# Holding the last three zero blocks until the last batch's ranks, half a weight matrix more ahead of the gathers, and a bank of its own for the score pieces

## The chip, the cores and the metric

The kernel runs on one core of one Trainium2 chip. The metric is the device time of one launch in microseconds (us), the median of several runs. The engines are named as in the profile: PE (TensorE), PEld (its weight loads), DVE (VectorE), ACT (ScalarE), POOL (GpSimd) and SP (SyncE, which here only issues DMAs). POOL issues DMAs too, into a queue of its own; all queues share the core's 16 DMA engines.

## The reference

```python
def reference(**kwargs):
    ...
    attn_out = _attn_ref(**attn_kwargs)
    B, H, S, D = attn_out.shape
    x = np.ascontiguousarray(attn_out.transpose(0, 2, 1, 3)).reshape(B * S, H * D)
    return _moe_ref(x=x, **moe_kwargs)
...
    logits = x @ w_gate
    expert_idx = np.argmax(logits, axis=1)
    ...
    gate_w = probs[np.arange(N), expert_idx]
    out = np.zeros((N, D), dtype=np.float32)
    for e in range(E):
        ...
        if len(tok_idx) > capacity:
            gw = gate_w[tok_idx]
            keep = np.argpartition(-gw, capacity)[:capacity]
            tok_idx = tok_idx[keep]
        h = np.maximum(x[tok_idx] @ w1[e], 0.0)
        out[tok_idx] = gate_w[tok_idx, None] * (h @ w2[e])
```

Attention for 8 batches of 8 heads: 512 local tokens that see a window of 32 to each side and 32 global tokens, and the global tokens, which see all. Its rows (4352 of 512 numbers) go to a mixture of 8 experts: each token goes to its best expert, an expert keeps the 80 tokens with the highest gate, and all other rows of the output are zero.

## The kernel before

The program is one list of operations (`op`), each with the resources that it reads and writes and a due time. A planner (`Work.emit`) sorts them by due time, by readiness under rough costs and by free PSUM banks, and so fixes the order of the instructions on each engine. The chip keeps only this order and the true dependences of tiles; a resource that is only a name in the list (such as "rk21") moves an operation in the order and makes nothing wait on the chip.

Attention fills the first 197 us, batch by batch (line 1030 on): scores, exponentials, values, normalisation (`norm`), rows cast to bf16 in `xb` and written to a scratch tensor `x_scr` (`X_rows`). Beside it `gate_pieces(b)` picks the tokens of each batch: logits, the one-hot of the best expert (`oh`), the score split into bf16 pieces (`v7`), a transpose of both into one PSUM bank (T56, line 718), from which rows 0:56 are copied to `oh3T` and rows 32:56 to `S3T`; then five products `r_ps` (line 736) whose signs or comparisons, summed, give the rank of each token in its expert. For the last batch DVE compares pieces 0 and 4 (line 745), and ACT counts signs of pieces 1, 2 and 3 (line 750) and turns the sums of signs into counts (line 756: half of it plus 256). `d_ps` does the same for the global tokens and gives `rk2` (line 771). `rank` and `ohs` (lines 778, 779) turn ranks into a one-hot, a product and a merge with the lists so far give `idx`, the 80 token numbers of each expert.

Then the experts' stage. POOL gathers the 80 rows of each expert by indirect DMA (`gather`, line 1090); PE transposes them (`f_turn`, line 1109), multiplies by w1 in two halves (`f_up`, line 1122) and by w2 (`f_down`, line 1139); ACT scales the result by the gate, POOL scatters it to `out` (line 1156). I call the four transposes of expert e fx-e, the halves of w1 up-e-a and up-e-b, and the product with w2 y-e.

Weights come as fp32 from HBM and are cast to bf16 by the DMA, 1 MB of bf16 per matrix, on POOL's queue, in the order in which POOL issues them, into buffers that attention has finished with. Those in `wload` (line 1027) are issued before the gathers; the last of them is the first half of w1 of expert 6. Those in `wlate` follow among the gathers (line 1171): seven halves, the second half of w1 of expert 6 between the gathers of experts 1 and 2.

Zeros: 17 blocks of 512 KB are written to `out` on SP's queue (`zero`, line 389), 14 between loads of v and the last three at the end of SP's list (line 1080). The scatters wait until all have landed.

`warm` (line 1183) puts matmuls that nobody reads (line 1190, "unread") into the gaps that the planner expects on PE in the end stage.

Of the kernel before, what the change touches and what calls it, by code (L numbers as in the profile page):

```python
# [76 lines left out]
class Work:  # L77
# [10 lines left out]
    def at(self, due):  # L88
        self.due = due
# [131 lines left out]
def kernel(  # L221
# [49 lines left out]
    def bankS(name, shape=(P, 512), dt=FP32):  # L271
        return Bank("S", list(shape), dt, name)
# [48 lines left out]
    ones = cp.tile([cap, 1], BF16, name="ones")  # L321
    gq32 = wr[2][:, 0:4096].bitcast(FP32).rearrange("p (t b x) -> p t b x", t=2, b=B)
# [295 lines left out]
    def gate_pieces(b):  # L618
# [99 lines left out]
        T56 = bankS(f"T56_{b}", (56, 544), BF16)  # L718
# [7 lines left out]
        op([("D", 0.45), ("A", 0.6)], lambda e: copy_on(e, oh3T[0:56, 0:544], T56[:]), rd=[T56],  # L726
           wr=["oh3T"])
        op([("A", 0.6), ("D", 0.45)], lambda e: copy_on(e, S3T[0:24], T56[32:56, :]), rd=[T56], wr=["S3T"])
        step = 1 if last else 2
        for u in range(5):  # L730
# [25 lines left out]
        op([("A", 0.25)], lambda e: nc.scalar.activation(  # L756
            out=st["rk1"][:, 1:4:step], in_=st["rk1"][:, 1:4:step], func=AF.Copy, scale=0.5, bias=256.0),
            rd=[f"rk1{y}{u}" for u in range(1, 4, step)], wr=[f"rk1{y}{u}" for u in range(1, 4, step)])
# [226 lines left out]
    def f(e):  # L985
# [5 lines left out]
                                                       op0=ALU.mult, op1=ALU.add), rd=["second"], wr=["wsg"])  # L991
    at(-50)
# [23 lines left out]
    for t_ in (1, 0):  # L1016
# [12 lines left out]
              (175, 6, 0, 0, 2)]  # L1029
    wlate = [(6, 0, 2, 4), (6, 1, 0, 4), (6, 1, 4, 8), (7, 0, 0, 2), (7, 0, 2, 4), (7, 1, 0, 4), (7, 1, 4, 8)]  # L1030
# [197 lines left out]
```

## Time and profile before

| | |
|---|---|
| median of 3 runs | 249.5 us (248.96 to 249.52) |
| the profiled execution | 248.41 us, its span 246.5 us |
| PE busy, of the span | 211.8 us, 86% |
| DVE, ACT, POOL busy | 155.8, 149.7, 130.5 us |
| DMA | 51.90 MB written, mean 211 GB/s |
| granted clock of PE, mean | 0.976 |

The span is the time from the first to the last instruction; the rest of the execution's own time lies around it. Busy shares are means over stages with different limits; the stage that matters here is read in stretches of one or two microseconds. GB/s counts the bytes written: a weight that is cast from fp32 to bf16 counts with its bf16 bytes.

### The profile page before, as it was taken

Reading aid. Unit: us, or ns where it says so; the run is one execution under the profiler, and the core shown is the slowest. Engines: PE = TensorE matmul, PEld = TensorE weight load, DVE = VectorE, ACT = ScalarE, POOL = GpSimd, SP = SyncE. Lnnn points to the kernel's source line nnn. Section 1 sums busy time; section 2 is a strip of 40 time slices with the busy share of each in tenths; the row PEclk is TensorE's granted clock in tenths of the full one; section 3 lists DMA queues with packets and bytes.
Section 4 is the critical chain, followed back from the end, with each engine's and each line's share of the span. In section 5 each row is a group of like instructions: output and inputs, shape, how many; then the busy total and the mean of one; then the engine's idle time right before and its main releaser. Section 6 shows DMA issues by size and latency. Waiting matters only on the chain.

```text
span 246.5 us, 10141 instructions
## 1 busy us (share of the span) xinstructions
PE 211.8 (86%) x4337; PEld 166.5 (68%) x4354; DVE 155.8 (63%) x396; ACT 149.7 (61%) x312; POOL 130.5 (53%) x215
## 2 busy tenths in 40 slices
PE   0589589797999898999799989999999977679991
PEld 0567477585778677887688768777778654357760
DVE  7248377718979857777676767878877777221210
ACT  2469557918878786867575878868593435024431
POOL 8937245525468564572547643516686330588331
PEclk9999979979999999999989999999999999999998
DMA  6999988999999999999997999997899999299971
GB/s 102 234 224 180 232 180 147 200 212 205 172 252 163 217 276 265 204 299 232 299 205 214 291 219 224 237 275 181 163 179 243 209 243 307 51 213 216 197 203 55
DMA packets 54798, 51.90 MB, mean 211 GB/s; under 512 B 42976, under 2 KB 43488, under 8 KB 53984
## 3 DMA queue, kind: packets, MB, share of 16 engines
q0 software_dynamic: 8896, 27.14, 59.6%
q1 hardware_dynamic: 45856, 24.11, 35.2%
q8 instruction: 34, 0.56, 0.9%
q14 instruction: 12, 0.10, 0.1%
HBM read 61.72 MB, written 14.68 MB: 310 GB/s over the span
## 4 chain that ended last, share of the span: by engine, by line
PE 60%; issue 13%; DVE 12%; POOL 7%; ACT 6%; POOLq 1%; DVEq 0%; ACTq 0%
PE o_ps L520 13%; PE o_ps L505 8%; PE T_ps L403 7%; PE x_ps L584 5%; PE l_ps L481 4%; PE lgT_ps L640 4%; PE r_ps L736 3%; PE og L551 3%; POOL out_dram L1156 2%; DVE qkT L266 2%; ACT eL L486 2%; PE T L723 2%; DVE xn L533 1%; PE Q_ps L460 1%; PE og L556 1%
## 5 line engine op out<-in xcount | busy, mean ns | idle before, releaser
L593 POOL CAST xb<-xn 128x512 bf16<-128x512 f32 x32 | 21.4, 669 | 44.2 <-DVE xn L533 36.8
L520 PE MATMUL o_ps<-vt,eL 128*64 128x65 f32 x1024 | 39.3, 231 | 3.0 <-issue 3.0
L486 ACT ACTIVATE eL<-l_ps 128x512 f32<-128x512 f32 x64 | 35.6, 609 | 5.5 <-PE l_ps L481 5.3
L520 PEld LDWEIGHTS o_ps<-vt,eL 128*64 128x64 f32 x1024 | 34.5, 143 | 6.6 <-issue 4.4
L491 DVE TENSOR_TENSOR eL<-eL,first 128x512 f32<-128x512 f32 x38 | 31.2, 844 | 7.5 <-ACT eL L486 7.3
L266 ACT COPY xT<-x_ps 128x512 f32<-128x512 f32 x30 | 17.6, 587 | 18.3 <-PE x_ps L584 18.3
L505 PE MATMUL o_ps<-vgb,eG 64*128 64x130 f32 x256 | 23.9, 303 | 4.4 <-issue 2.4
L533 DVE TENSOR_TENSOR xn<-o_ps,rec 128x512 f32<-128x512 f32 x32 | 22.1, 692 | 3.1
L505 PEld LDWEIGHTS o_ps<-vgb,eG 64*128 64x128 f32 x256 | 17.7, 190 | 8.3 <-issue 4.7
L266 ACT COPY qkT<-T_ps 128x1024 f16<-128x1024 f16 x21 | 21.4, 1020 | 3.0 <-PE T_ps L403 3.0
L266 POOL COPY vt<-vt 64x260 f32<-64x260 f32 (+2 forms) x30 | 22.1, 750 | 1.9 <-DMA vt<-in_v_l_dram 0.6
L403 PE MATMUL T_ps<-ident,qk 128*64 128x128 f16 x512 | 22.1, 239 | 0.1
L266 DVE COPY qkT<-T_ps 128x1024 f16<-128x1024 f16 x11 | 13.5, 1224 | 12.0 <-PE T_ps L403 11.9
L584 PE MATMUL x_ps<-identf,xn 128*128 128x128 f32 x128 | 20.4, 283 | 0.4
L403 PEld LDWEIGHTS <-qk 128*64 128x64 f16 x512 | 18.0, 122 | 1.9 <-issue 1.0
L584 PEld LDWEIGHTS x_ps<-identf,xn 128*128 128x128 f32 x128 | 15.2, 143 | 2.9
L481 PE MATMUL l_ps<-qkT 64*128 64x64 f16 x512 | 14.5, 198 | 2.7 <-DVE qkT L266 1.9
L266 ACT COPY vt<-vt 64x1040 f32<-64x1040 f32 (+2 forms) x18 | 16.1, 900 | 0.5 <-DMA vt<-in_v_l_dram 0.2
L491 POOL TENSOR_TENSOR eL<-eL,first 128x512 f32<-128x512 f32 x10 | 12.0, 1198 | 7.7 <-ACT eL L486 5.9
L481 PEld LDWEIGHTS <-qkT 64*128 64x128 f16 x512 | 10.8, 99 | 7.7 <-issue 4.1
L745 DVE SCALAR_TENSOR_TENSOR junk<-r_ps,second 128x512 bf16<-128x512 f32 x23 | 15.6, 680 | 0.5 <-PE r_ps L736 0.5
L532 DVE RECIPROCAL rec<-o_ps 128x8 f32<-128x8 f32 x32 | 6.4, 201 | 13.3 <-PE o_ps L520 13.2
(174 smaller groups left out, 444.5 us busy)
## 6 DMA issues: line engine op xcount, KB each, us to landing
out_dram<-zt SPq DMA_DIRECT2D x17, 512.0 KB, 9.7
vt<-in_v_l_dram SPq DMA_DIRECT2D x64, 128.0 KB, 4.9
wr<-in_moe_w_dram POOLq DMA_DIRECT2D x6, 1024.0 KB, 9.9
qk<-in_q_l_dram POOLq DMA_DIRECT2D x8, 512.0 KB, 7.4
qk<-in_k_l_dram POOLq DMA_DIRECT2D x8, 512.0 KB, 7.6
x_scr<-xb SPq DMA_DIRECT2D x8, 512.0 KB, 7.8
qk<-in_moe_w_dram POOLq DMA_DIRECT2D x2, 1024.0 KB, 11.2
qkT<-in_moe_w_dram POOLq DMA_DIRECT2D x2, 1024.0 KB, 9.6
```

The lines of the kernel that those rows point to most:

```text
L266: (eng.copy if e == "A" else eng.tensor_copy)(out=out, in_=in_)
L403: nc.tensor.transpose(out=bk[64 * q:64 * q + 64, i, :], in_=qk16[b % 2][:, t, q, 8 * half + i, :], identity=ident16[:, :])
L481: mm(out=lps[s, k][:, 64 * t:64 * t + 64], lhsT=kv(s, j)[r, 64 * t:64 * t + 128], rhs=qv(s, j)[r, 64 * t + 32:64 * t + 96], start=k != 2, ...
L486: op([("A", 0.53)], lambda e, k=k, e_=e_: nc.scalar.activation(out=e_, in_=lps[s, k][:], func=AF.Exp, scale=scale), rd=[lps[s, k]], wr=[f" ...
L491: lambda e, e_=e_: engines[e].tensor_tensor(out=e_, in0=e_, in1=band, op=ALU.mult),
L505: mm(out=o[:, j, 130 * u:130 * u + 130], lhsT=eG[s % 2][r, q0:q0 + 128], rhs=vgb[r, s // 2, s % 2].rearrange("p h d -> p (h d)"), start=(u ...
L520: mm(out=ost[s, h][64 * odd:64 * odd + 64, k // 2, c:c + 65], lhsT=eL[s % 2][:, k, 64 * t:64 * t + 64], rhs=v[:, 4 * odd + u, k, :], start ...
L533: nc.vector.tensor_tensor(out=xn[:, s % 2, h].rearrange("p j u (k d) -> p j (u k) d", k=2), in0=o[:, :, :, 0:64], in1=rec[:].unsqueeze(3). ...
L584: nc.tensor.transpose(out=bk[:, c:c + 128], in_=xn[:, s % 2, h, j, u], identity=identf[:, :])
L593: op([("G", 0.65)], lambda e: nc.gpsimd.tensor_copy(out=xb[(s // 2) % 2][:, 2 * h:2 * h + 2, :, s % 2, :].rearrange("p u q (j d) -> p u q ...
L640: mm(out=lgt[32 * c:32 * c + 32, 0:P], lhsT=wg[:, f, :], rhs=xslot(2 * b + f // 2, c, f % 2), start=(f == 0), stop=(f == 3), skip_group_ch ...
L745: nc.vector.scalar_tensor_tensor(out=junk[:], in0=bk[:], scalar=0.0, in1=wst[:, 512 - 128 * u:1024 - 128 * u], op0=ALU.add, op1=ALU.is_gt, ...
```

## The change

- The last three zero blocks are to start later: SP first issues a DMA of 4 bytes (`word`) from `rk2` of the last batch, so that SP waits for it, and behind it the three blocks.
- The list ahead of the gathers takes the whole of w1 of expert 6. Six halves stay among the gathers, at other places.
- For the last batch the pieces of the score are transposed a second time, into a bank of their own (T24), from which `S3T` is copied by ACT, while DVE copies `oh3T` from T56.
- For the last batch the sums of signs are no longer turned into counts: `rk2` of columns 1 to 3 is doubled on DVE (line 786 of the changed kernel), and `ohs` compares with a table `rev5`, whose columns 1 to 3 hold 2 x - 512. Two operations on POOL make the table early on.
- `df` is kept in bf16 in all batches.

```diff
@@ gate_pieces @@
-        T56 = bankS(f"T56_{b}", (56, 544), BF16)
+        T24 = T56 = bankS(f"T56_{b}", (56, 544), BF16)
+        r24 = slice(32, 56)
+        if last:
+            T24, r24 = bankS(f"T24_{b}", (24, 544), BF16), slice(0, 24)
+
+            def f(e):
+                for u in range(5):
+                    n = P if u < 4 else SG
+                    nc.tensor.transpose(out=T24[:, 128 * u:128 * u + n], in_=st["vi"][0:n, u, 32:56],
+                                        identity=identb[0:n, 0:n])
+            op([("P", 0.3)], f, rd=["v7" + y, "identb"], new=[T24], mode="128x56", tail=0.2, room=1)
...
-        op([("A", 0.6), ("D", 0.45)], lambda e: copy_on(e, S3T[0:24], T56[32:56, :]), rd=[T56], wr=["S3T"])
-        step = 1 if last else 2
+        op([("A", 0.6)] if last else [("A", 0.6), ("D", 0.45)], lambda e: copy_on(e, S3T[0:24], T24[r24, :]), rd=[T24], wr=["S3T"])
...
-        op([("A", 0.25)], lambda e: nc.scalar.activation(
-            out=st["rk1"][:, 1:4:step], in_=st["rk1"][:, 1:4:step], func=AF.Copy, scale=0.5, bias=256.0),
+        if not last:
+            op([("A", 0.25)], lambda e: nc.scalar.activation(
+            out=st["rk1"][:, 1:4:2], in_=st["rk1"][:, 1:4:2], func=AF.Copy, scale=0.5, bias=256.0),
...
-            df = t("df", [P, 5, SG])
+            df = t("df", [P, 5, SG], BF16)
...
+            if last:
+                nc.vector.tensor_scalar(out=st["rk2"][:, 1:4], in0=st["rk2"][:, 1:4], scalar1=2.0, scalar2=None, op0=ALU.mult)
...
-            nc.vector.tensor_tensor(out=ohs[:], in0=(nat if b == 0 else rev).unsqueeze(1).to_broadcast([P, 5, cap]),
+            nc.vector.tensor_tensor(out=ohs[:], in0=rev5[:] if last else (nat if b == 0 else rev).unsqueeze(1).to_broadcast([P, 5, cap]),
@@ the constants @@
+        nc.gpsimd.tensor_copy(out=rev5[:, 0:5:4], in_=rev.unsqueeze(1).to_broadcast([P, 2, cap]))
+        nc.gpsimd.tensor_scalar(out=rev5[:, 1:4], in0=rev.unsqueeze(1).to_broadcast([P, 3, cap]), scalar1=2.0, scalar2=-512.0,
+                                op0=ALU.mult, op1=ALU.add)
+    op([("G", 0.9)], f, rd=["second"], wr=["rev5"])
@@ the weights @@
-              (175, 6, 0, 0, 2)]
-    wlate = [(6, 0, 2, 4), (6, 1, 0, 4), (6, 1, 4, 8), (7, 0, 0, 2), (7, 0, 2, 4), (7, 1, 0, 4), (7, 1, 4, 8)]
+              (175, 6, 0, 0, 4)]
+    wlate = [(6, 1, 0, 4), (6, 1, 4, 8), (7, 0, 0, 2), (7, 0, 2, 4), (7, 1, 0, 4), (7, 1, 4, 8)]
...
+    at(119)
+    op([("S", 0.4)], lambda e: nc.sync.dma_start(out=word[:], in_=fin["rk2"][0:1, 0:1]), rd=["rk21"], wr=["word"], dma=0.02)
     for i in range(14, 17):
-        zero(i, 100, "rk21")
+        zero(i, 119.1, "word")
...
-        for i in {1: (0,), 3: (1,), 5: (2,), 7: (3, 4, 5, 6)}.get(e, ()):
+        for i in {2: (0,), 4: (1,), 7: (2, 3, 4, 5)}.get(e, ()):
```

On POOL at the gathers, before (`kbd` and `qbd` hold the gathered rows of experts 0 to 3 and 4 to 7, `vt_83`, `eL_86`, `eL_87` and `xn` are the places of w1 of expert 6, w2 of 6, w1 of 7 and w2 of 7; the first row is the last of the score pieces):

```order
L709 TENSOR_TENSOR vi_4364<-r_4379,vi_4364 128x5x8
L1090 DMA kbd<-x_scr,idx 80x512 x2
L383 DMA vt_83<-in_moe_w_dram 128x2048
L1090 DMA kbd<-x_scr,idx 80x512 x2
L380 DMA eL_86<-in_moe_w_dram 128x2048
L1090 DMA qbd<-x_scr,idx 80x512 x2
L380 DMA eL_86<-in_moe_w_dram 128x2048
L1090 DMA qbd<-x_scr,idx 80x512 x2
L383 DMA eL_87<-in_moe_w_dram 128x2048 x2
L380 DMA xn<-in_moe_w_dram 128x2048 x2
```

and in the changed kernel:

```order
L711 TENSOR_TENSOR vi_4368<-r_4383,vi_4368 128x5x8
L1115 DMA kbd<-x_scr,idx 80x512 x3
L382 DMA eL_86<-in_moe_w_dram 128x2048
L1115 DMA kbd<-x_scr,idx 80x512
L1115 DMA qbd<-x_scr,idx 80x512
L382 DMA eL_86<-in_moe_w_dram 128x2048
L1115 DMA qbd<-x_scr,idx 80x512 x3
L385 DMA eL_87<-in_moe_w_dram 128x2048 x2
L382 DMA xn<-in_moe_w_dram 128x2048 x2
L1181 DMA out_dram<-xb_98,idx 4352x512 x2
```

The gather of expert 2 now follows that of expert 1 at once, and the load that stood between them is gone; the load that stood behind expert 3 stands ahead of it.

On DVE, the ranks of the last batch, before (`more`, `oh_109`: the merge of the lists of batch 6; `junk`: the comparisons of pieces 0 and 4):

```order
L266 COPY oh3T<-T_7_4394 56x544
L837 TENSOR_TENSOR more<-D_ps_0_4401,second 80x320
L837 TENSOR_TENSOR more<-D_ps_1_4409,second 80x320
L770 TENSOR_TENSOR df_4428<-d_ps_4416,second 128x160
L771 TENSOR_REDUCE rk_4430<-df_4428 128x5
L745 SCALAR_TENSOR_TENSOR junk,rk_124<-r_ps_0_4422,second 128x512
L745 SCALAR_TENSOR_TENSOR junk,rk_124<-r_ps_4_4441,second 128x512
L847 TENSOR_TENSOR oh_109<-second,rs_ps_4444 80x640
L778 TENSOR_TENSOR rank_4459<-rk_124,rk_4430 128x5
L779 TENSOR_TENSOR ohs<-second,rank_4459 128x400
```

and in the changed kernel:

```order
L266 COPY oh3T<-T_7_4405 56x544
L852 TENSOR_TENSOR more<-D_ps_0_4412,second 80x320
L852 TENSOR_TENSOR more<-D_ps_1_4419,second 80x320
L782 TENSOR_TENSOR df_4438<-d_ps_4426,second 128x160
L784 TENSOR_REDUCE rk_4440<-df_4438 128x5
L786 TENSOR_SCALAR rk_4440<-rk_4440 128x3
L756 SCALAR_TENSOR_TENSOR junk,rk_126<-r_ps_0_4432,second 128x512
L756 SCALAR_TENSOR_TENSOR junk,rk_126<-r_ps_4_4452,second 128x512
L862 TENSOR_TENSOR oh_109<-second,rs_ps_4455 80x640
L793 TENSOR_TENSOR rank_4468<-rk_126,rk_4440 128x5
L794 TENSOR_TENSOR ohs<-rev_117,rank_4468 128x400
```

The doubling of `rk2` is new, ahead of the two comparisons; all else stands as before, the merge's `oh_109` ahead of `rank` too.

On PE, where expert 2's and expert 3's rows are first needed, before (the rows ahead are the last of up-1-b; the eight transposes of experts 2 and 3 stand together, the first five of them here, and y-1 follows the last):

```order
L1122 MATMUL h_ps_1_4601<-eQ_91,wr_101 128x80
L1109 LDWEIGHTS kbd
L1109 MATMUL fx_ps_4619<-first,kbd 128x80
L1109 LDWEIGHTS kbd
L1109 MATMUL fx_ps_4619<-first,kbd 128x80
L1109 LDWEIGHTS kbd
L1109 MATMUL fx_ps_4619<-first,kbd 128x80
L1109 LDWEIGHTS kbd
L1109 MATMUL fx_ps_4619<-first,kbd 128x80
L1109 LDWEIGHTS kbd
L1109 MATMUL fx_ps_4625<-first,kbd 128x80
L1109 LDWEIGHTS kbd
```

and in the changed kernel (the rows ahead are the last of up-2-a, then fx-3, then y-1):

```order
L1147 LDWEIGHTS wr_102
L1147 MATMUL h_ps_0_4636<-eQ_90,wr_102 128x80
L1134 LDWEIGHTS kbd
L1134 MATMUL fx_ps_4654<-first,kbd 128x80
L1134 LDWEIGHTS kbd
L1134 MATMUL fx_ps_4654<-first,kbd 128x80
L1134 LDWEIGHTS kbd
L1134 MATMUL fx_ps_4654<-first,kbd 128x80
L1134 LDWEIGHTS kbd
L1134 MATMUL fx_ps_4654<-first,kbd 128x80
L1164 LDWEIGHTS eG_89
L1164 MATMUL y_ps_4659<-wr_101,eG_89 80x512
```

The transposes of expert 2 have moved forward, ahead of y-0, and up-2-a now stands ahead of fx-3 and y-1. Further back an "unread" matmul that stood after the transposes of expert 5 is gone.

## Rows read from the trace of the kernel before

**Rows 1.** Windows of the run's last third; columns: stretch, length, busy time per engine, clock, DMA share, GB/s.

```profile
206.00:208.00 2.00, 2.00 (x17) 0.90 (x14) 1.55 (x6) 1.84 (x5) 0.00 (x0) 1.00 1.02 399
...
210.00:212.00 2.00, 2.00 (x10) 0.77 (x8) 0.91 (x7) 0.00 (x0) 0.86 (x1) 1.00 0.04 14
...
214.00:216.00 2.00, 1.80 (x37) 1.42 (x37) 0.65 (x2) 0.44 (x1) 1.39 (x3) 1.00 0.73 107
216.00:218.00 2.00, 2.00 (x33) 1.48 (x30) 0.00 (x0) 0.87 (x2) 1.69 (x3) 1.00 1.01 201
...
220.63:236.00 15.37, 15.31 (x219) 11.28 (x221) 3.24 (x9) 5.55 (x11) 8.88 (x11) 1.00 1.03 200
```

**Rows 2.** Timeline of PE, experts' stage: start us, length us, line, operation, count, [idle before <-releaser].

```profile
213.86 0.33 PE L1109 MATMUL fx_ps<-first,kbd 80*128 80x80 bf16 x4 [1.77 <-DMA kbd<-x_scr,idx]
...
216.77 1.90 PE L1139 MATMUL y_ps<-wr,eG 128*80 128x512 bf16 x8
218.50 0.74 PE L1122 MATMUL h_ps<-eQ,wr 128*128 128x80 bf16 x16
220.63 0.49 PE L1109 MATMUL fx_ps<-first,kbd 80*128 80x80 bf16 x8 [1.39 <-DMA kbd<-x_scr,idx]
220.95 1.90 PE L1139 MATMUL y_ps<-wr,eG 128*80 128x512 bf16 x8
...
228.59 0.74 PE L1122 MATMUL h_ps<-eQ,qkT 128*128 128x80 bf16 x16
229.16 0.31 PE L1109 MATMUL fx_ps<-first,qbd 80*128 80x80 bf16 x4
229.52 0.74 PE L1122 MATMUL h_ps<-eQ,qkT 128*128 128x80 bf16 x16
...
239.28 1.89 PE L1139 MATMUL y_ps<-xn,eG 128*80 128x512 bf16 x8
```

**Rows 3.** Timeline of POOL, first gathers and the load among them.

```profile
211.14 1.08 POOL L1090 DMA_INDIRECT kbd<-x_scr,idx  x1 [7.76 <-DVE mv L813]
212.53 0.97 POOL L1090 DMA_INDIRECT kbd<-x_scr,idx  x1 [0.31 <-issue]
213.51 0.61 POOL L383 DMA_DIRECT2D vt<-in_moe_w_dram  x1
214.42 1.00 POOL L1090 DMA_INDIRECT kbd<-x_scr,idx  x1 [0.30 <-issue]
```

**Rows 4.** Timelines of PE (first row) and ACT, the last batch's ranks.

```profile
203.44 0.53 PE L723 MATMUL T<-first,vi 128*56 128x128 bf16 x5 [0.34 <-POOL vi L709]
...
204.47 0.60 ACT L266 COPY S3T<-T 24x544 bf16<-24x544 bf16 x1 [2.51 <-DVE oh3T L266]
...
208.25 0.20 ACT L756 ACTIVATE rk<-rk 128x3 f32<-128x3 f32 x1
```

**Rows 5.** Timeline of DVE, the last batch's ranks.

```profile
204.42 0.88 DVE L837 TENSOR_TENSOR more<-D_ps,second 80x320 bf16<-80x320 f32 x2
205.44 0.32 DVE L770 TENSOR_TENSOR df<-d_ps,second 128x160 f32<-128x160 f32 x1
205.80 0.32 DVE L771 TENSOR_REDUCE rk<-df 128x5 f32<-128x160 f32 x1
...
207.18 0.69 DVE L745 SCALAR_TENSOR_TENSOR junk<-r_ps,second 128x512 bf16<-128x512 f32 x1 [0.45 <-PE r_ps L736]
...
208.53 0.15 DVE L778 TENSOR_TENSOR rank<-rk,rk 128x5 f32<-128x5 f32 x1
```

**Rows 6.** Timeline of SP: the last three zero blocks.

```profile
197.93 1.85 SPq L391 DMA_DIRECT2D out_dram<-zt  x3
```

**Rows 7.** DMA issues of the last 67 us: count, KB each, median us to landing.

```profile
eL<-in_moe_w_dram POOLq DMA_DIRECT2D x4, 512.0 KB, 6.1
```

**Rows 8.** Timeline of POOL where the new operations go in.

```profile
44.92 1.83 POOL L978 TENSOR_SCALAR nown<-second 128x640 bf16<-128x640 bf16 x1
...
49.16 0.61 POOL L593 CAST xb<-xn 128x512 bf16<-128x512 f32 x1 [1.52 <-DVE xn L533]
```

More of the change, by code (lines that the diff above doesn't have):

```diff
@@ L321 @@
     ones = cp.tile([cap, 1], BF16, name="ones")
+    word = cp.tile([1, 1], FP32, name="word")
+    rev5 = cp.tile([P, 5, cap], BF16, name="rev5")
     gq32 = wr[2][:, 0:4096].bitcast(FP32).rearrange("p (t b x) -> p t b x", t=2, b=B)
@@ L725, in gate_pieces @@
         op([("P", 0.3)], f, rd=["vi" + y, "v7" + y, "identb"], new=[T56], mode="128x56", tail=0.2, room=1)
-        op([("D", 0.45), ("A", 0.6)], lambda e: copy_on(e, oh3T[0:56, 0:544], T56[:]), rd=[T56],
+        op([("D", 0.45)] if last else [("D", 0.45), ("A", 0.6)], lambda e: copy_on(e, oh3T[0:56, 0:544], T56[:]), rd=[T56],
            wr=["oh3T"])
-        op([("A", 0.6), ("D", 0.45)], lambda e: copy_on(e, S3T[0:24], T56[32:56, :]), rd=[T56], wr=["S3T"])
-        step = 1 if last else 2
+        op([("A", 0.6)] if last else [("A", 0.6), ("D", 0.45)], lambda e: copy_on(e, S3T[0:24], T24[r24, :]), rd=[T24], wr=["S3T"])
         for u in range(5):
@@ L754, in gate_pieces @@
                 op([("D", 0.87)], f, rd=[bk, "second"], wr=[f"rk1{y}{u}"])
-        op([("A", 0.25)], lambda e: nc.scalar.activation(
-            out=st["rk1"][:, 1:4:step], in_=st["rk1"][:, 1:4:step], func=AF.Copy, scale=0.5, bias=256.0),
-            rd=[f"rk1{y}{u}" for u in range(1, 4, step)], wr=[f"rk1{y}{u}" for u in range(1, 4, step)])
+        if not last:
+            op([("A", 0.25)], lambda e: nc.scalar.activation(
+            out=st["rk1"][:, 1:4:2], in_=st["rk1"][:, 1:4:2], func=AF.Copy, scale=0.5, bias=256.0),
+            rd=[f"rk1{y}{u}" for u in range(1, 4, 2)], wr=[f"rk1{y}{u}" for u in range(1, 4, 2)])
         at(s0 + 17)
@@ L768, in f @@
         def f(e):
-            df = t("df", [P, 5, SG])
+            df = t("df", [P, 5, SG], BF16)
             nc.vector.tensor_tensor(out=df[:], in0=d[:], in1=wgl, op=ALU.is_gt)
-            nc.vector.tensor_reduce(out=t("rk2", [P, 5])[:], in_=df[:], axis=AX.X, op=ALU.add)
+            fin["rk2"] = t("rk2", [P, 5])
+            nc.vector.tensor_reduce(out=st["rk2"][:], in_=df[:], axis=AX.X, op=ALU.add)
+            if last:
+                nc.vector.tensor_scalar(out=st["rk2"][:, 1:4], in0=st["rk2"][:, 1:4], scalar1=2.0, scalar2=None, op0=ALU.mult)
         op([("D", 0.75)], f, rd=[d, "second"], wr=["rk2" + y])
@@ L778, in f @@
             nc.vector.tensor_tensor(out=rank[:], in0=st["rk1"][:], in1=st["rk2"][:], op=ALU.add)
-            nc.vector.tensor_tensor(out=ohs[:], in0=(nat if b == 0 else rev).unsqueeze(1).to_broadcast([P, 5, cap]),
+            nc.vector.tensor_tensor(out=ohs[:], in0=rev5[:] if last else (nat if b == 0 else rev).unsqueeze(1).to_broadcast([P, 5, cap]),
                                     in1=rank[:].unsqueeze(2).to_broadcast([P, 5, cap]), op=ALU.is_equal)
-        op([("D", 0.8)], f, rd=[f"rk1{y}{u}" for u in range(5)] + ["rk2" + y, "second"], wr=["ohs"])
+        op([("D", 0.8)], f, rd=[f"rk1{y}{u}" for u in range(5)] + ["rk2" + y, "second"] + (["rev5"] if last else []), wr=["ohs"])
         Bb = bankS(f"B_ps{b}", (cap, 7, 8))
@@ L991, with f @@
                                                        op0=ALU.mult, op1=ALU.add), rd=["second"], wr=["wsg"])
+    def f(e):
+        nc.gpsimd.tensor_copy(out=rev5[:, 0:5:4], in_=rev.unsqueeze(1).to_broadcast([P, 2, cap]))
+        nc.gpsimd.tensor_scalar(out=rev5[:, 1:4], in0=rev.unsqueeze(1).to_broadcast([P, 3, cap]), scalar1=2.0, scalar2=-512.0,
+                                op0=ALU.mult, op1=ALU.add)
+    op([("G", 0.9)], f, rd=["second"], wr=["rev5"])
     at(-50)
```

## The prediction

> **What bounds the kernel now.** I read the page first (PE busy for 86% of the span), then the windows of the last third, then the timelines of PE, POOL and DVE there; no other stretch holds a changed order. The reader should see three things.
>
> First, PE ends the run. [...] Ahead of that PE stands idle for 1.39 us by the profile, from the end of up-1-b until the gathered rows of experts 2 and 3 land at 220.63 [rows 2].
>
> Second, why they land so late: POOL issues the gather of expert 2 at 214.42, behind a 512 KB load at 213.51, and its data queue behind that load [rows 3]. The gather of expert 0, with an empty queue, needed 2.72 us from issue (211.14) to the transposes that use it (213.86) [rows 2, 3].
>
> Third, the DMA engines are idle just before: 14 GB/s from 210 to 212 us [rows 1]. The zeros (issued from 197.93 on [rows 6]) have been written by then beside the last weights, with 399 GB/s from 206 to 208 [rows 1].
>
> **The change, part by part.**
>
> *The load ahead of the gathers.* It adds 0.52 MB to what must land before the gathers; at 201 GB/s, the rate of loads from 216 to 218 [rows 1], that is 2.6 us. The stretch has room: nothing flows from 210 to the first gather, whose data move shortly before 213.86. The issue on POOL stays one instruction. So this costs nothing on the path; if its cover (the idle 210 to 213) were gone, the gathers would slip by up to 2.6 us.
>
> *The zeros.* Three blocks are 1.57 MB, 3.9 us at 399 GB/s. Held back, they leave these 3.9 us to the weights, which then land near 210 - 3.9 + 2.6 = 209. On SP only the zeros stand behind the new 4-byte DMA, and only the scatters wait for the zeros. `rk2` is ready when its reduce ends, 0.68 us after `df` starts (205.44 and 205.80 + 0.32 [rows 5]), near 206.5 in the changed order. Issuing takes 1.85 us for three blocks [rows 6], a third of that at most for the small one, so the first block is issued near 207.1. Its data begin between at once and 2.7 us later (a gather's issue to landing), so the zeros end between 211.0 and 213.7; I take 212.2, nearer the early end, since the 2.72 us contain a gather's data too. They fill the idle stretch and cost nothing, unless they end late (a rival, below).
>
> *The ranks.* The second set of five transposes delays T56 by 0.53 us at most [rows 4]; I take 0.5. `S3T` no longer waits for DVE's copy (that wait ended ACT's idle time before 204.47 [rows 4]), and the 0.20 us of ACT at 208.25 go. Both shorten ACT's side, but DVE is just as late: `rank` starts at 208.53, when DVE comes to it. DVE gets T56 0.5 us later and has the doubling in addition: 0.15 us by `rank`, of the same size, up to 0.47 if it also waits out the reduce of 0.32 [rows 5]. Its slack is 0.14 us ahead of `df` (204.42 + 0.88 against 205.44) and 0.45 ahead of the last comparison [rows 5]. 0.5 + 0.15 - 0.59 = 0.06 later; ends: 0.2 earlier (ACT's row, were DVE's additions free) and 0.4 later. I take 0.05 later.
>
> `df` in bf16 could shorten the reduce. The fp32 one takes 0.32 us for 160 numbers [rows 5]; no row shows one in bf16, so it stays in the sum with the same time. [...]
>
> *rev5 on POOL.* 400 numbers per partition; by `nown` (1.83 us for 640) at most 1.15 us, below that nothing to speak of, once, where POOL then idles for 1.52 us waiting for DVE [rows 8]. Hidden at both ends.
>
> *The experts' stage.* This is the term. With gathers 0, 1 and 2 in a row, 1.39 us apart [rows 3], gather 2 is issued near 213.9 and lands near 216.6, before fx-2 is due at 216.77 (the start of y-0 before [rows 2]). PE then runs on: fx-2 0.15 us (229.16 to 229.52 holds one such group and one unread matmul of 0.21, an eighth of a y), y-0 1.73 (216.77 to 218.50), up-1-b and up-2-a 0.57 each (228.59 to 229.16), and reaches fx-3 at 219.80 [rows 2]. Gather 3 is the next late thing: it now stands behind a load. Call L the time at which its rows can be used. After it come fx-3 (0.17) and y-1; from y-1 to y-7 it took 239.28 - 220.95 = 18.33 us [rows 2], less up-2-a (0.57), done already, and the unread matmul (0.21) gone: 17.55. So y-7 starts at L + 17.72, the gain is 221.56 - L, and cannot exceed 1.76 (L = 219.80).
>
> L is bounded from both sides. That load is issued near 213.92 + 0.98 = 214.90 (0.98 from a gather to the load behind it [rows 3]). Lower end: the time of a gather on an empty queue and 2.6 us for the load: 214.90 + 2.72 + 2.6 = 220.2. Upper end: what it took before from the issue of the load (213.51) to the rows of expert 2 (220.63), 7.12 us: 222.0. The first load of before ran slowly (107 GB/s from 214 to 216, against 201 after [rows 1]). The load that now takes its place, the first half of w2 of expert 6, landed 6.1 us after issue with a load and two gathers ahead of it [rows 7], so that I do not expect the whole of the slowness again. I take L = 220.75, a third of the way up: a gain of 0.81. Everything behind is ahead of need: one load fewer is in the queue, and it was no bound before (PE did not wait after 220.63).
>
> **Sum:** 0.81 - 0.05 = 0.76, say 0.8 us. The profiled execution took 248.4 us (span 246.5); it would take 247.6. The median of the runs lies 1.1 above it, at 249.5, so the forecast is **248.7 us**.
>
> **The rivals.** About 0.3%, 0.75 us, is what a measurement can tell from no change.
>
> - *No new wait* (0.15): gather 3 lands before PE comes to it at 219.80. Gain 1.76, less the 0.05 of the ranks: 247.8. For: the queue is short then. Against: even the lower end of L is 0.4 above that.
> - *The wait only moves* (0.22): gather 3 is as late behind its load as gather 2 was, L = 222.0. Loss 0.44 and the 0.05 of the ranks: 250.0, within the band of no change; with L above 221.3, under 0.3 is gained. For: the same kind of load starts on the same empty queue. Against: only one gather, not two, has to follow.
> - *Slower, by the zeros* (0.10): their last bytes still move when the gathers of experts 0 to 2 start. Place: the DMA engines at 212 to 215. Price: in a loaded queue a gather pays for its share; if the first gather is held by 2.6 us (one half-matrix time), fx-0 starts at 216.5, PE runs without a wait from there (6.11 us from fx-0 to y-1: 213.86 to 219.80 and fx-3), y-1 starts at 222.6 and y-7 at 240.1: 0.85 slower, 250.3. It decides from the point at which the zeros end after 213, that is with data starting over 2 us after issue. Against: by my middle they end at 212.2. [...] No row before shows gathers beside zeros.
> - That the hold does nothing: SP's wait is real (the 4 bytes are data of DVE), and 3.9 us of zeros can't be hidden elsewhere; if it did fail, zeros and weights would end at 210 + 2.6 = 212.6, still before the gathers. So it is priced within the forecast.
>
> **How the numbers follow.** The forecast, a new and shorter wait for gather 3 (gain 0.3 to 1.3), has 0.53. Of that about 0.32 lies above 0.75; with the first rival, faster has 0.47. Slower by over 0.3% is the zeros' case and a little of the second: 0.10. The rest, 0.43, is no change. The range reaches from the first rival (247.8) to the second (250.0), and leaves out the zeros' case.
>
> **What would show it.** Right: in the changed profile the transposes of expert 2 stand ahead of y-0 without a wait; PE waits once, for fx-3, between 219.8 and 221.5; y-7 starts near 238.5; `rank` stays within 0.2 us of 208.5; the DMA engines write near 400 GB/s between 208 and 212. Wrong: fx-0 later than 214.5 (zeros or weights in the way), `rank` later than 208.9, or a wait for fx-3 that lasts beyond 221.6.

## The result and the profile after

Four runs of the changed kernel took 251.13 to 252.89 us, median 252.32, beside four of the kernel before, 248.96 to 253.88, with a median of 249.51. The ratio is 1.0114, with a 95% interval of 1.0065 to 1.0163: 1.1% slower by this comparison. (The comparison's own ratio leaves out each run over 1.5% above the fastest of its kernel, here the 253.88 us of the kernel before; since the runs of any of these kernels turned out to spread over more than that without a gap, I give means and ranges of all runs below, and the own ratio beside them.) The means of all eight runs differ by 1.7 ± 2.4 us, an interval that holds zero. Forecast were 248.7 us and a range of 247.8 to 250.0.

The profiled execution took 251.13 us (span 249.3, mean granted clock 0.963), against 248.41 (246.5, 0.976) before. This table splits the 2.7 us between the spans (246.54 and 249.26 in the trace) by the starts of five rows; those of before are in [rows 2 to 5].

| stretch | before | after | difference |
|---|---|---|---|
| start to the first transposes of the last score pieces | 203.44 | 206.54 | +3.10 |
| these to `mv` (ranks, merge, lists) | 7.42 | 7.47 | +0.05 |
| `mv` to the issue of gather 0 | 0.28 | 0.53 | +0.25 |
| gather 0 to fx-0 | 2.72 | 2.73 | +0.01 |
| fx-0 to y-7 | 25.42 | 24.75 | -0.67 |
| y-7 to the end | 7.26 | 7.24 | -0.02 |

So all of the loss had happened ahead of the last batch's ranks, where the order of PE, ACT and DVE first differs, and what the change is about gained 0.3 to 0.4 us.

PE in the experts' stage of the changed kernel (timeline: start, length, operation, idle before it and releaser), which answers to [rows 2]:

```profile
217.27 0.33 PE L1134 MATMUL fx_ps<-first,kbd 80*128 80x80 bf16 x4 [2.02 <-DMA kbd<-x_scr,idx]
...
220.11 0.31 PE L1134 MATMUL fx_ps<-first,kbd 80*128 80x80 bf16 x4
220.26 1.89 PE L1164 MATMUL y_ps<-wr,eG 128*80 128x512 bf16 x8
...
224.37 0.33 PE L1134 MATMUL fx_ps<-first,kbd 80*128 80x80 bf16 x4 [1.07 <-DMA kbd<-x_scr,idx]
...
242.02 1.89 PE L1164 MATMUL y_ps<-xn,eG 128*80 128x512 bf16 x8
```

fx-2 stands ahead of y-0 without a wait; PE waits once, 1.07 us, for fx-3, and fx-3 starts 7.10 us after fx-0. In the prediction's time (fx-0 at 213.86) that is L = 220.96; 220.75 was taken.

DVE (first two rows), SP and POOL of the changed kernel, answering to [rows 3, 5, 6]:

```profile
211.68 0.15 DVE L793 TENSOR_TENSOR rank<-rk,rk 128x5 f32<-128x5 f32 x1
...
214.01 0.16 DVE L828 TENSOR_TENSOR mv<-Rv,bv 80x8 f32<-80x8 f32 x1
```

```profile
209.45 0.71 SPq L1104 DMA_DIRECT2D word<-rk  x1
210.54 2.09 SPq L393 DMA_DIRECT2D out_dram<-zt  x3
```

```profile
214.54 1.08 POOL L1115 DMA_INDIRECT kbd<-x_scr,idx  x1 [8.06 <-DVE mv L828]
...
218.16 0.62 POOL L382 DMA_DIRECT2D eL<-in_moe_w_dram  x1
219.08 1.01 POOL L1115 DMA_INDIRECT kbd<-x_scr,idx  x1 [0.30 <-issue]
```

`rank` is 3.15 us later than before [rows 5], where its inputs are 3.10 later. Gather 0 goes out 0.37 us after the end of `mv` (214.17); before it was 0.12. The zeros were still flowing then (windows of the changed kernel; the last number is GB/s); whether they are what held it is answered behind the fourth batch.

```profile
212.00:214.00 2.00, 2.00 (x19) 1.06 (x18) 1.50 (x8) 0.40 (x1) 0.00 (x0) 1.00 1.03 418
214.00:216.00 2.00, 1.25 (x6) 0.39 (x4) 0.17 (x3) 0.00 (x0) 1.16 (x2) 1.00 0.63 256
```

And this is where most of the 3.10 us came in: PE inside attention, with the same instructions in the same order. First the changed kernel, timeline and window (the clock is the third number from the end), then the same stretch of the kernel before.

```profile
97.34 0.37 PE L558 MATMUL og<-vgb,egg 64*32 64x65 f32 x8 [2.06 <-issue]
...
97.34:110.90 13.56, 13.56 (x244) 10.89 (x243) 8.04 (x21) 8.40 (x18) 5.74 (x10) 0.75 1.00 240
```

```profile
97.90 0.32 PE L556 MATMUL og<-vgb,egg 64*32 64x65 f32 x8 [1.03 <-issue]
...
97.90:108.61 10.71, 10.56 (x243) 8.71 (x243) 7.97 (x22) 8.39 (x19) 6.67 (x12) 1.00 1.02 226
```

PE stands still for 2.06 us (before: 1.03) and waits for nothing that the profile shows. Behind that the mean clock is 0.75, that is half of the 13.56 us at 0.50 (97.50 to 104.30, and 1.00 from there on, by windows); before it was 1.00. This stretch alone is 2.85 us longer. PE stopped 1.59 us earlier than before ahead of it (95.28 against 96.87) and is 2.29 us later behind it; elsewhere the two differ by smaller steps both ways. The question for the experiments was whether the change did that.

### The profile page after: what moved, and what is told of

It reads as the page before. It is cut to its first block, busy times and chain, and to the rows that moved or that the text cites. A ratio compares the mean times of both kernels' runs of the same rounds, so it can differ in the third digit from the quotient of the medians.

```text
span 249.3 us, 10171 instructions
## 1 busy us (share of the span) xinstructions
PE 213.7 (86%) x4358; PEld 167.1 (67%) x4358; DVE 155.1 (62%) x398; ACT 149.3 (60%) x310; POOL 129.8 (52%) x216
## 4 chain that ended last, share of the span: by engine, by line
PE 53%; issue 14%; DMA 8%; DVE 7%; ACT 6%; POOL 6%; SPq 4%; POOLq 1%; ACTq 0%; DVEq 0%
PE o_ps L522 12%; PE o_ps L507 7%; PE x_ps L586 4%; PE T_ps L405 4%; DMA vt<-in_v_l_dram 4%; PE lgT_ps L642 3%; PE r_ps L747 3%; PE l_ps L483 3%; PE og L553 3%; POOL out_dram L1181 2%; ACT eL L488 2%; DMA eL<-in_moe_w_dram 2%; DMA vgb<-in_v_g_dram 2%; SPq L952 2%; SPq L365 2%
## 5 line engine op out<-in xcount | busy, mean ns | idle before, releaser
L522 PE MATMUL o_ps<-vt,eL 128*64 128x65 f32 x1024 | 39.8, 233 | 1.7 <-issue 1.7
L522 PEld LDWEIGHTS o_ps<-vt,eL 128*64 128x64 f32 x1024 | 35.1, 145 | 5.3 <-issue 3.1
L493 DVE TENSOR_TENSOR eL<-eL,first 128x512 f32<-128x512 f32 x38 | 30.0, 812 | 9.0 <-ACT eL L488 8.8
L266 POOL COPY vt<-vt 64x260 f32<-64x260 f32 (+2 forms) x30 | 21.1, 718 | 7.2 <-PE T_ps L405 3.8
L747 PE MATMUL r_ps<-S3T,oh3T 128*128 128x512 bf16 x40 | 15.1, 381 | 0.0
```

What stands on the lines that cost most here:

```text
L493: lambda e, e_=e_: engines[e].tensor_tensor(out=e_, in0=e_, in1=band, op=ALU.mult),
L522: mm(out=ost[s, h][64 * odd:64 * odd + 64, k // 2, c:c + 65], lhsT=eL[s % 2][:, k, 64 * t:64 * t + 64], rhs=v[:, 4 * odd + u, k, :], start ...
L747: mm(out=bk[:], lhsT=oh3T[:, 128 * u:128 * u + 128], rhs=S3T[:, 0:512], start=True, stop=not soft)
```

## The experiments

Theory A: the change loses time upstream by something it does early (`rev5`, `df`, the load that goes ahead). Theory Z: zeros and gathers collide. Theory N, later S: nothing was lost; executions of one kernel are spread in attention, and four against four caught a bad draw. The kernels of one batch ran on one chip and share its runs of the kernel before. Means stand with 95% intervals from the spread of the runs (1.96 standard errors, which is too narrow for six runs).

### First batch: the whole again, and its parts alone

*copy*: no edit.

> The changed kernel as it is, once more. Theory A (the loss is made upstream of the gathers, by what the change does early or to the timing there): about 252 us, fx-0 some 3 us later than in the kernel before, the extra time gathered before 130 us, and again a stretch of clock 0.50 in other places than before (97.5 to 104.3 in the first profile). Theory N (the first comparison caught a bad draw of runs, and the two kernels differ by less than 1 us): 248.5 to 250 us. Theory Z (zeros and gathers collide): about 252, but all of it after 205 us.

*early*: the kernel before with two edits:

```diff
-            df = t("df", [P, 5, SG])
+            df = t("df", [P, 5, SG], BF16)
+        nc.gpsimd.tensor_copy(out=rev5[:, 0:5:4], in_=rev.unsqueeze(1).to_broadcast([P, 2, cap]))
+        nc.gpsimd.tensor_scalar(out=rev5[:, 1:4], ...
```

> The kernel before with only the early parts of the change: df in bf16 and the two POOL operations that fill rev5, which nobody reads here. Theory A in the form that rev5 or df moves attention: 2 to 3.5 us slower than before, about 252. If A holds but comes from another part, or under N or Z: within 0.75 us of the kernel before.

*ranks*: the changed kernel with the zeros and loads of before (`df` stays in bf16 here):

```diff
-    op([("S", 0.4)], lambda e: nc.sync.dma_start(out=word[:], in_=fin["rk2"][0:1, 0:1]), ...
-        zero(i, 119.1, "word")
+        zero(i, 100, "rk21")
-              (175, 6, 0, 0, 4)]
+              (175, 6, 0, 0, 2)]
-        for i in {2: (0,), 4: (1,), 7: (2, 3, 4, 5)}.get(e, ()):
+        for i in {1: (0,), 3: (1,), 5: (2,), 7: (3, 4, 5, 6)}.get(e, ()):
```

> The changed kernel without its zeros and loads (three zero blocks at once as before, the second half of w1 of expert 6 among the gathers as before): early parts and ranks. Theory A by rev5 or df: about 252, like the changed kernel plus the 0.6 us that its experts' stage gains, so up to 253. Theory Z or N: within 0.75 us of the kernel before, since by the rows of the first profile rank was 3.15 us later where everything was 3.1 us later.

*loads*: the kernel before with these lines of the change alone (the `word` DMA, the held zeros, the lists `wload` and `wlate`, the places among the gathers).

> The kernel before with only the held zero blocks and the loads at their new places; no rev5, df in fp32, ranks as before. Theory A by rev5 or df: faster than before by the 0.6 us that the experts' stage gained in the first profile (248.9). Theory Z: the loss stays, about 252. If the loss is made upstream by the load that goes ahead of the gathers (it shares the DMA engines with attention's loads): about 252, the time lost before 200 us.

| kernel | runs | mean, us | lowest to highest | mean against before | own ratio and its interval |
|---|---|---|---|---|---|
| before | 29 | 249.8 | 246.3 to 252.8 | | |
| copy | 13 | 250.1 | 245.3 to 255.3 | +0.3 ± 1.9 | 0.993 (0.986 to 1.001) |
| early | 12 | 251.8 | 246.7 to 256.9 | +2.0 ± 2.0 | 0.995 (0.989 to 1.001) |
| ranks | 12 | 251.4 | 247.3 to 254.6 | +1.6 ± 1.6 | 1.000 (0.995 to 1.006) |
| loads | 6 | 253.4 | 251.2 to 256.5 | +3.6 ± 1.8 | 1.015 (1.007 to 1.023) |

One and the same program now took 245.3 to 255.3 us. The whole change was not slower, but by the means of all runs each of its parts seemed to be (by the own ratio only loads), which can't be by a cause in the parts unless they undo each other. None of the theories had this table; it made draws the first suspect.

### Second batch: the kernel before against itself, and the end stage

*before2*: the kernel before, no edit.

> The kernel before itself, once more, compared with itself. Theory S (the executions of one and the same kernel are spread over several us in attention, and the 2.8 us of the first comparison were a draw): runs between 246 and 253 us, median within 1 us of the other runs of the same kernel; fx-0 in the profile anywhere from 212 to 217, but from the start of the last og group of attention to fx-0 again 20.4 us, and from fx-0 to y-7 25.4 (no draw in the end stage). Theory A (the changed kernels are slower in attention for a cause of their own): tight, 249.0 to 250.5, fx-0 at 213.9.

*copy2*: the changed kernel, no edit.

> The changed kernel a third time. Theory S: median 249 to 250.5, no more than 0.5 us from before, runs from 245 to 255; in the end stage again 20.8 us from the last og group to fx-0 and 24.8 from there to y-7, together 0.3 less than before. Theory A: again some 252, the copy's 249.9 having been the odd draw.

*nohold*: the changed kernel without the `word` DMA, `zero(i, 100, "rk21")` as before.

> The changed kernel with the three zero blocks issued at once, as before, and no 4-byte DMA. If the held zeros delay the first gather (it was issued 0.37 us after mv in both profiles of the changed kernel, 0.12 to 0.13 in those without the hold): 0.13 here, and the last og group to fx-0 takes 20.5 us. If the hold is needed to free the engines for the weights: the last weights land 2 to 3 us later and the gathers with them, fx-0 2 us later after mv than the 3.3 us seen. The time of the whole by theory S: 249 to 251.

*g3first*: the changed kernel with one line changed.

```diff
-        for i in {2: (0,), 4: (1,), 7: (2, 3, 4, 5)}.get(e, ()):
+        for i in {3: (0,), 5: (1,), 7: (2, 3, 4, 5)}.get(e, ()):
```

> The changed kernel with the first half of w2 of expert 6 issued behind the gather of expert 3 instead of ahead of it, the second half behind that of expert 5. If the wait for fx-3 (1.07 us in the profile of the changed kernel) is that load: no wait for fx-3, and from fx-0 to y-7 23.7 us instead of 24.8. If another thing holds the gather (its place in POOL's queue): the wait stays. The whole by theory S: 1.0 us less than the changed kernel, within the spread of the runs.

The kernel before, 11 shared runs and 6 of before2, took 246.3 to 259.9 us, more than the whole range of the first comparison. copy2 had a mean of 250.2 (6 runs), nohold 251.3, g3first 251.0, against 251.7 of these 17: none can be told apart (own ratios of before2, copy2 and nohold 1.006, 1.000 and 1.001, with intervals that hold 1). My expectation for before2 that the end stage has no draws was wrong: from the last og group to fx-0 it took 21.9 us, not 20.4, since a stretch of clock 0.50 lay on the ranks (window from the transposes to `mv`; clock 0.81):

```profile
203.81:212.67 8.86, 7.61 (x58) 3.99 (x60) 5.70 (x20) 3.28 (x9) 0.00 (x0) 0.81 0.65 227
```

nohold was to tell whether the held zeros delay gather 0. It went out 0.13 us after `mv`, as expected without a hold, but the ranks of this profile, too, ran at a mean clock of 0.81 (and so did those of best, below), and so late that gather 0 came 0.12 to 0.14 after `mv` with the hold as well (copy2, copy3, copy4). So nohold answers nothing here.

In g3first PE comes to fx-3 without a wait, as expected, but fell into clock 0.50 some 1.8 us behind fx-0 (210.38), so that fx-0 to y-7 took 26.33 us and not 23.7:

```profile
212.38:214.38 2.00, 1.52 (x24) 1.34 (x22) 0.33 (x1) 0.44 (x1) 1.69 (x3) 0.50 0.34 66
...
218.84 0.31 PE L1134 MATMUL fx_ps<-first,kbd 80*128 80x80 bf16 x4
```

### Third batch: what the draws are

Each profile has the waits of PE "for nothing" at the same few matmuls, some 127 matmuls or a multiple of that apart, counted in PE's timeline, with lengths that differ by execution. *shift64* moves PE's instructions along without changing the work:

```diff
+            if t and b0 == 0:
+                for _ in range(64):
+                    nc.tensor.transpose(out=bk[:, 0, 0:16], in_=ident16[0:16, :], identity=ident16[0:16, 0:16])
```

> The changed kernel with 64 more small transposes, which nobody reads, ahead of PE's first one, so that every later PE instruction stands 64 matmuls and 64 weight loads further on in the program; the work and its order are the same. In eight of nine profiles so far that have the row, PE stands still for 0.8 to 3.1 us, waiting for nothing that the profile shows, at one and the same matmul, the first og<-vgb,egg of the seventh stage; the other such stalls stand 127 or 254 matmuls apart. Theory F (PE waits for its own next block of instructions, some 127 matmuls and as many weight loads long): no stall there; instead one 64 matmuls earlier, inside the group lgT_ps<-xT (near 95 us), and likewise the one ahead of o_ps<-vgb,eG near 122 to 128 us goes to lgT_ps<-xgT. Theory D (PE waits there for data that the profile does not name): the stall stays at og<-vgb,egg, with 1 to 3 us. The time of the whole: within the spread of the changed kernel's runs by both.

*copy3*: the changed kernel, no edit.

> The changed kernel once more, to set the spread of its runs against that of the kernel before. If the two differ only by draws: median of all its runs within 1 us of that of all runs of the kernel before (250 so far). End stage: without a stretch of clock 0.50 in it, 7.4 to 7.5 us from the transposes of the last score pieces to mv, and 24.8 from fx-0 to y-7.

*best*: the edits of nohold and g3first together.

> The changed kernel without the hold (three zero blocks issued at once, no 4-byte DMA) and with the first half of w2 of expert 6 behind the gather of expert 3. By the rows so far: gather 0 issued 0.13 us after mv, no wait for fx-3, and from fx-0 to y-7 23.8 us where no stretch of clock 0.50 falls in, 1.6 less than the kernel before. If the weights do not land in time without the hold: gather 0 still 0.13 after mv, but fx-0 more than 2.9 us after its issue. The whole: 248 to 250 us, median up to 1.5 us below before, less than one run differs from the next.

*shift127*, run after these: `range(127)` in place of `range(64)`.

> As with 64 more transposes, but with 127, the distance at which the stalls of the other profiles stand from each other. Theory F (PE waits for its next block of instructions): the limits of the blocks fall on the same matmuls of the work as without any, so PE stands still again ahead of the first og<-vgb,egg of the seventh stage, 0.8 to 3.1 us, and ahead of o_ps<-vgb,eG in the tenth; all of its waits for nothing between 20 and 200 us add up to 4 to 11 us, as in the kernels without a shift, and not to the 2.4 us of the shift by 64. If instead the 64 transposes took the stall away in another manner (by a later start, or by what they do to the clock): no stall there with 127 either.

The og group of the seventh stage in four profiles (timeline of PE), copy, before2, shift64 and shift127:

```profile
102.65 0.32 PE L558 MATMUL og<-vgb,egg 64*32 64x65 f32 x8 [3.07 <-issue]
```

```profile
99.80 0.32 PE L556 MATMUL og<-vgb,egg 64*32 64x65 f32 x8 [1.02 <-issue]
```

```profile
101.84 0.32 PE L558 MATMUL og<-vgb,egg 64*32 64x65 f32 x8
```

```profile
97.85 0.24 PE L558 MATMUL og<-vgb,egg 64*32 64x65 f32 x1
101.09 0.32 PE L558 MATMUL og<-vgb,egg 64*32 64x65 f32 x7 [3.00 <-issue]
```

With 64 more transposes the wait is gone; with 127 it is back, 3.00 us, one matmul further on. So it belongs to a place in the program and not to the data of the work: theory F. In shift127 PE also waits ahead of `o_ps` in the tenth stage, 0.66 us, as expected. One of the page's DMA queues goes with it, here its row of the changed kernel and that of shift127 (packets, MB, share of the engines' time):

```profile
q8 instruction: 34, 0.56, 0.8%
```

```profile
q8 instruction: 35, 0.57, 0.9%
```

The 34 packets have 0.56 MB together, 16.5 KB each, and the changed kernel's page counts 4358 matmuls and as many weight loads on PE: 8716 / 34 is, by an estimate from these counts, 256 instructions of PE to a packet, where the places of the waits stand 254 apart. 127 pairs more make one packet more. What sets the length of the wait, 0.8 to 3.1 us in this og group, these rows do not show.

The packets themselves show the link more directly. In the changed kernel PE stops at 95.28 and goes on at 97.34, and one of them starts between 95.1 and 95.2 (DMA queues of that window):

```profile
q8 instruction: 1, 0.02, 58.4%
```

All 110 such waits of the 17 profiles between 20 and 200 us (without two of 0.16 us ahead of unread matmuls) ended 2.2 to 3.0 us after the start of one of these packets, which come some 6 us apart. So the end of these waits goes with the start of a packet; that PE waits for the instructions in it is theory F's reading, since the traces name no releaser. One expectation of F missed: no wait appeared 64 matmuls earlier, in `lgT_ps`. But the three waits that shift64 does have stand with 732, 1366 and 1494 weight loads ahead of them, where other profiles have theirs (731 in early, 1366 in copy2, 1494 in before), at other work: the places stayed in the program, and at a place the wait can also be nothing. All waits for nothing between 20 and 200 us add up to 2.4 us in shift64, to 5.7 in shift127 and to 4.3 to 10.7 in the others (waits of PE). Yet shift64 was not faster: 255.7 on a mean of 10 runs, 3.2 ± 2.8 above before (own ratio 1.010, 1.004 to 1.017), with 5.2 us of waiting for a late `vt` in its profile. shift127 took 251.9 and 261.0 us, before in that batch 245.0 to 252.1. I draw nothing from these times.

copy3 (12 runs) had a mean of 251.8, best (12) 252.0, the kernel before on that chip 252.5 (29): -0.7 ± 2.0 and -0.5 ± 2.2 (own ratios 1.004 and 1.000). The 248 to 250 us expected of best were missed with the kernel before itself at 252.5. In the profile of best no gather is waited for behind fx-0; fx-0 to y-7 took 24.78 us, of which 0.66 is a wait for DVE that I had not expected:

```profile
216.78 0.77 PE L1144 MATMUL h_ps<-eQ,wr 128*128 128x80 bf16 x16 [0.66 <-DVE eQ L1134]
...
220.40 0.31 PE L1131 MATMUL fx_ps<-first,kbd 80*128 80x80 bf16 x4
...
238.39 1.89 PE L1161 MATMUL y_ps<-xn,eG 128*80 128x512 bf16 x8
```

### Fourth batch: do the parts have a cause of their own

*early2* and *loads2* are early and loads once more, *copy4* the changed kernel.

> The early parts alone (rev5 on POOL, df in bf16) once more. If they cost attention time by themselves: again some 2 us above the kernel before, and above the copy of the whole change by no less than the 0.3 that its end stage gains. If the 2.0 us were a draw: mean within 1.5 us of the kernel before on this chip. End stage in the profile as in the kernel before: 7.42 us from the last transposes to mv where the clock is 1.00 (8.8 to 8.9 with a stretch of 0.50), gather 0 at 0.13 after mv, 25.2 to 25.5 from fx-0 to y-7.

> The held zeros and the loads alone once more. If the hold costs time: gather 0 issued 0.25 to 0.75 us after mv where the ranks ran at clock 1.00, PE still for over 1.9 us ahead of fx-0 and, as in three of five such profiles, 3.4 us of clock 0.50 behind it; mean 1 us or more above the kernel before and above the copy of the whole. If the 3.6 us were a draw: mean within 1.5 us of the kernel before on this chip. Where the ranks fall into a stretch of 0.50: gather 0 at 0.13 after mv and no low clock at fx-0.

> The changed kernel once more, on the chip of the two others. By draws alone: mean within 1.5 us of the kernel before, below or above, in no fixed order with the other two. If the first comparison had shown a cause: 2 to 3 us above the kernel before.

| kernel | runs | mean, us | lowest to highest | mean against before | own ratio and its interval |
|---|---|---|---|---|---|
| before | 23 | 249.9 | 245.1 to 255.0 | | |
| early2 | 12 | 250.0 | 245.6 to 254.7 | +0.1 ± 2.1 | 0.996 (0.990 to 1.002) |
| loads2 | 12 | 249.9 | 246.6 to 254.6 | +0.1 ± 1.8 | 1.004 (0.999 to 1.009) |
| copy4 | 6 | 248.5 | 243.2 to 257.4 | -1.4 ± 4.2 | |

The +2.0 and +3.6 of the first batch did not come back. They ran on another chip there, so a cost on that chip alone is not excluded. Over the batches that ran both kernels, the kernel before ran 102 times (245.1 to 259.9, median 250.65), the changed one 41 times (243.2 to 258.6, median 250.21). Taken chip by chip and weighted, the difference of the means is 0.0 ± 1.1 us (-0.5 ± 1.2 without the first comparison). The 2.8 us between the medians of the first comparison were a draw; an effect of some 1 us either way is not excluded.

The end stage, in all 17 profiles (us; from start to start, but `mv` to gather 0 from the end of `mv`; the fourth column is the time from the end of an instruction of POOL, `drain`, to gather 0):

| profile | transposes to `mv` | transposes to the landing of the last weights ahead | `drain` to gather 0 | `mv` to gather 0 | fx-0 to y-7 |
|---|---|---|---|---|---|
| before, early, early2 | 7.42, 7.42, 7.42 | 4.79, 3.67, 3.64 | 1.68, 2.79, 2.82 | 0.12, 0.13, 0.13 | 25.42, 25.18, 25.32 |
| before2 | 8.86 (clock 0.81) | 3.55 | 4.36 | 0.13 | 26.23 |
| ranks | 7.48 | 3.77 | 2.75 | 0.13 | 25.54 |
| loads, loads2 | 7.42, 9.07 (0.81) | 5.79, 6.00 | 1.14, 2.12 | 0.60, 0.13 | 25.77, 24.83 |
| after, copy | 7.47, 7.47 | 5.62, 5.62 | 1.14, 1.14 | 0.37, 0.37 | 24.75, 24.78 |
| copy2, copy3, copy4 | 8.84, 8.90, 8.85 (0.81) | 6.47, 5.75, 5.83 | 1.42, 2.19, 2.06 | 0.13, 0.13, 0.12 | 24.93, 25.00, 24.61 |
| nohold, best | 8.86, 8.82 (0.81) | 5.98, 5.49 | 1.94, 2.38 | 0.13, 0.13 | 24.92, 24.78 |
| g3first, shift127 | 7.48, 7.48 | 5.52, 5.99 | 1.14, 1.14 | 0.26, 0.75 | 26.33, 25.10 |
| shift64 | 8.89 (0.81) | 5.54 | 2.39 | 0.14 | 25.76 |

The mean clock from fx-0 to y-7 was 0.93 or 0.94 in early2, loads, g3first and shift127, else 1.00. Three readings follow. The changed ranks cost 0.05 to 0.06 us (7.47 and 7.48 against 7.42). Gather 0 is late by 0.13 to 0.62 us in each profile of a held kernel whose ranks ran at full clock (0.26 to 0.75 against 0.13), and in no other. And the moved gathers gain: of the profiles at full clock, and without the waits of PE behind fx-0 that are neither gathers nor the first `eQ` (before2 has 1.2 us of them, shift64 1.7, best 0.8), those with the moved gathers took 24.75, 24.78, 24.93, 25.00, 24.61, 24.92 and 24.83 us (mean 24.83), the others 25.42, 25.18 and 25.54 (mean 25.38).

What makes gather 0 late is not the zeros. Both kernels have a `nc.gpsimd.drain()` on POOL between the weights ahead of the gathers and gather 0 (line 1170 before, 1195 after); a timeline leaves it out, its line shows it (shortest, median and longest length in ns, then the first and the last start in us), first before, then after:

```profile
L1170 POOLq DRAIN  x1: 6378/6378/6378, 203.1 to 203.1; - x1
```

```profile
L1195 POOLq DRAIN  x1: 7218/7218/7218, 206.2 to 206.2; - x1
```

In all 17 profiles the drain ends 1.24 to 1.25 us after the last weight load that POOL issued ahead of it has landed, and gather 0 goes out either 0.13 us after `mv` or 1.14 us after the drain, whichever is later. The five late ones are the five at 1.14. The load that was moved ahead puts that landing off: to 5.49 to 6.47 us after the transposes in the twelve profiles that have it there, with the hold or without it (nohold, best), against 3.55 to 4.79 in the five that don't. The ranks at clock 0.81 hide it, since `mv` then comes 1.4 us later; in copy2 zeros flowed until 0.76 us behind the issue of gather 0, and it was not late. With ranks at full clock, by an estimate from the same two distances, gather 0 of nohold would be 0.6 us late and that of best 0.1; no profile shows the load ahead without the hold in that case.

## Why the prediction was wrong, and where it held

- **"No other stretch holds a changed order"**, and the sum made from there, is where it failed, with "0.3% is what a measurement can tell". The first is true, but I took from it that the stretch up to the ranks lasts the same in every execution. Three runs within 0.56 us and a profile 1.1 below their median were all I had; the 102 runs show a spread of 15 us for the same program. A range of 2.2 us could not hold that, whatever the change did. The term that was missing is the stretch ahead of the ranks: copy and copy4 are one program, and their transposes of the last score pieces start at 209.66 and 199.25 us. In that difference are PE's waits for nothing (8.6 us against 6.1 between 20 and 200 us), 6.8 us at clock 0.50 against none, and a wait of 3.6 us for a late `vt` against none.
- **Ranks, +0.05**: held, +0.05. The doubling took 0.17 us (0.15 was taken). The reduce of bf16 took 0.32 us, the same as in fp32 [rows 5].
- **Experts' stage, -0.81**: the mechanism held, fx-2 without a wait and one new wait for fx-3; the size was -0.67 in the first pair and -0.55 between the means of the table. L was 0.2 us later than taken.
- **The load ahead of the gathers "costs nothing on the path"**: failed, by 0.25 us in the first pair and 0.13 to 0.62 in the five profiles at full clock. The sum counted the DMA engines and left out POOL's `drain`, which takes 1.24 us from the landing of these weights to its end and 1.14 more to gather 0. The landing came at 209.06 in the prediction's time (less 3.10), where 209 was forecast, but by luck: before, the last weights landed at 208.23 and not near 210, the load added 1.9 us and not 2.6 (means of the table, 5.80 against 3.88), and the 3.9 us that the hold was to leave to the weights show nowhere.
- **The hold costs nothing**: no run shows a cost, and none a gain. The zeros were issued at 207.44 in the prediction's time (210.54 less 3.10; 207.1 was taken) and still flowed when gather 0 was due. The rival's price, a gather slowed in the queue, did not come: from issue to fx-0 it took 2.66 to 2.81 us in all 17 profiles. But its case was not met either: the zeros' last packet ended at most 1.46 us after the issue of gather 0, and POOL's queue moved its first packet for the gather 1.8 us after it.
- **`rev5`, 0**: held. early2 and copy4 show no cost that can be told from none.
- **"Slower" as the zeros' case**: the first comparison fell there, but not by this mechanism, which would have put the loss behind 205 us.

By the rows, the change is worth some -0.3 us (0.05 + 0.25 - 0.67 = -0.37 in the first pair), and -0.5 where slow ranks hide the wait for the drain. The runs can neither confirm nor refute so small a gain. best, which was to be rid of both new waits, can't be told from either kernel by its times.

Left open: why a packet of queue 8 starts late, why DVE comes late to fx-1 in before2, best and g3first, and whether the longer standstill ahead of fx-0 where gather 0 is late (1.94 to 2.37 us in the five such profiles, 1.71 to 1.86 in the others) brings the clock down there. It fell in three of these five, but in early2 too, after 1.80.

## What to carry to other kernels

Before a sum of tenths is set against a median, find out how far executions of the unchanged kernel differ; a few that agree may be luck, and four runs against three, with a fourth left out for being far off, gave an interval that excluded zero for an effect that 41 against 102 runs don't show. The run left out was the first sign of the spread. When the time changes, line up equal instructions of both profiles: a difference that is already there ahead of the first moved instruction is no proof against the change, but it has to be shown again in a copy before a cause is looked for. Local terms, read between two fixed rows, can be settled to 0.05 us even where the whole can't. And when a transfer starts late, read every instruction of the queue that issues it: here, in all 17 profiles, a drain ended 1.24 to 1.25 us after the landing of the last weights loaded ahead of the first gather, which went out no earlier than 1.14 us after that. An experiment that leaves one suspect out, as nohold did, answers nothing where something else hides the delay.

## What the runs showed of the hardware

- PE stood still in the middle of a stage without a releaser in the profile: 0.8 to 3.1 us at the first matmuls of one og group in 13 of the 15 profiles without a shift, and at other matmuls some 254 instructions or a multiple of that away. All 110 such waits between 20 and 200 us ended 2.2 to 3.0 us after the start of a packet of queue 8. With 128 more instructions ahead the wait at this og group was gone, and with 254 more it was back, 3.00 us, one matmul on.
- Stretches of clock 0.50 fell at other places in each profile of the changed kernel (by windows of 1 us, up to 240 us: 29 to 36, 97 to 105 and 124 to 129 us in after, 62 to 66 and 103 to 107 in copy, 75 to 79, 126 to 130 and 208 to 212 in copy2, 30 to 37, 149 to 154 and 207 to 212 in copy3, 200 to 205 in copy4), some of them right behind a standstill of PE (2.06 us ahead of that from 97.50 in after); with such a stretch in them the ranks took 1.4 us longer (8.85 against 7.47).
- POOL's `drain` ended 1.24 to 1.25 us after the landing of the last weight load that POOL had issued ahead of it, in all 17 profiles, and the gather behind it went out no earlier than 1.14 us after that.
